# Four PSUM banks for scores and relu, three for maxima, with new orders; the last head projected with the last tile

## The chip, the cores and the metric

The kernel runs on one core of one Trainium2 chip. The metric is the device time of one execution in microseconds. PE stands for TensorE's matmuls and PEld for its weight loads, DVE for VectorE, ACT for ScalarE, POOL for GpSimd, and SP for the engine that issues most DMAs.

## The reference, cut to what matters

```python
def _A_ref(x, wqkv, wo):            # 32 heads, each with its own k and v, Dh = 18
    qkv = (x @ wqkv).reshape(B, S, 3, H, Dh)          # S = 2048, D = 576
    p = softmax(q k^T * Dh ** -0.5); o = p v
    return o.reshape(B, S, D) @ wo
def _B_ref(x, wq, wk, wv, wo):      # 32 heads of q, one k and one v for all
    ...
g = sigmoid((x * gate_w).sum(-1, keepdims=True))
return g * _A_ref(x, ...) + (1 - g) * _B_ref(x, ...)
```

Both parts see the same x. In the kernel they are 64 heads in a row: heads 0 to 31 are the B part, with k from ksb and v from vb, and heads 32 to 63 the A part, with k from ksa or ksb and v from vg.

## The kernel before, in words

The order of all instructions on each engine is the order in which the program is written out (a manual schedule). Tiles in PSUM come from pools that hand out banks in turn: ps_s with three banks (tiles ps), ps_m with four (tiles pm), and ps_o with the one bank acc. An instruction that writes a bank waits until the bank's last reader is done.

*First phase.* x and the weights are split into a high and a low part, and 56 projections (14 tiles of 128 weight columns by 4 stretches of 512 rows of x, `project`) of 14 matmuls each go to PSUM, three in ps and three in pm by turns, and are evicted to DRAM scaled by tv. `balance` works out tv from the sizes of the weights by a transpose (br to pm) and a small matmul (bd, two) on TensorE, once for the B part and once for the A part; `turn_mask` transposes a mask that it needs, and `shared_v` transposes v of the B part. `split_x` prepares further stretches of x. Then project_v makes v of the A part, beside the maxima of the first rows (the order LEADS).

*Second phase.* The loop runs over T in steps of two; T // 16 is the head, T % 16 the first of two tiles of 128 keys, A and B. A pass of the loop does for both tiles the scores of 4 stretches of 512 queries (sA0 to sB3, `step_scores`, 56 rows at partition 0, exponentials on ScalarE), the maxima of another head's rows 22 tiles ahead (mA0 to mB3, `step_max`, 54 rows at partition 64, reductions on VectorE), and the product of the exponentials of the pass before with v (`step_pv`, four matmuls of 19 columns side by side in acc): P or p and f for tile A, Q or h and H for tile B, whole (512 queries) or in halves of 256. Of the eight maxima of a pass one (mA1) is left out: x is a matmul with the difference of two stretches of k, ScalarE takes its relu, and VectorE adds it to mA0's scores and takes the maximum in one instruction (L519). x is made one pass ahead. So ScalarE reads nine tiles a pass, and VectorE seven. U is a unit of the output projection (`out_proj`): twelve matmuls of 288 columns into one bank, which ScalarE copies (first segment) or VectorE adds to oacc (later ones).

A pass takes one order string. Before a head's first pass, M and T stand at different heads: the row maxima of a head are put together by `max_rows` on VectorE ahead of the pass with T % 16 = 10. In the pass with T % 16 = 0 (END) the last product of a head is done and `head_out` copies acc on VectorE; the next pass is AFTER, and others are PLAIN. A pass with a unit due is UNIT, wherever it stands. ALONE is for the last passes (T from 1002), when no maxima are left.

Units come in segments: 32 units of the first four tiles of 128 rows of the heads' outputs (T 521 to 857, one or two a head), 32 of the next four (T 942 to 1008), and 32 short ones of three matmuls for the 110 rows of the ninth tile (T from 1021, the rest behind the loop). The last head's 18 rows are projected by `last_out`: acc is copied and split, stacked by DMAs into 54 rows, and multiplied in 32 matmuls, scaled by the reciprocal sums while VectorE adds to oacc. The rows of out leave by DMA, 16 in all.

## Time and profile before

| | |
|---|---|
| median of 3 runs | 2694.31 us (2694.18 to 2694.47) |
| the profiled execution's own time | 2694.18 us |
| its span in the profile | 2692.4 us |
| busy PE, DVE, ACT, POOL | 99%, 90%, 89%, 10% of the span |
| granted TensorE clock | 0.997, mean |
| stretch 300 to 1300 us: busy DVE, ACT | 98.1%, 98.8% |
| stretch 1432 to 2193 us: busy DVE, ACT | 93.5%, 95.7% |
| stretch 2449 to 2589 us: busy DVE, ACT | 83.7%, 80.3% |

The first two rows and the span are read together: the time of an execution lies 1.8 us over the span that its instructions fill. A busy share of PE of 99% says little, since matmuls are pipelined and their ends are modelled; start-to-start times say more. In rows of a timeline the columns are start, duration (us), engine, line, operation, output and inputs with shapes, count, and the idle time before with what ended it. In a chain of waits they are start, duration, and engine with what it did.

### The profile page before, as it was taken

How to read it: one execution, taken by the hardware profiler on the slowest of the kernel's cores; microseconds unless marked ns; L12 is line 12 of the kernel's file. 1: busy time of each engine (PE TensorE's matmuls, PEld its weight loads, DVE VectorE, ACT ScalarE, POOL GpSimd, SP SyncE). 2: the span in 40 equal slices, each digit the busy share in tenths (PEclk: the TensorE clock that was granted, in tenths of full speed). 3: DMA queues.
4: the chain of work that ended last, by engine and by line, in shares of the span. 5: the costliest groups of instructions: out<-in, count | busy, mean ns of one | idle time of the engine just before them, and what ended most of it. 6: DMA issues, size and time to landing. Idle time of an engine off the chain costs nothing.

```text
span 2692.4 us, 57950 instructions
## 1 busy us (share of the span) xinstructions
PE 2658.4 (99%) x22210; PEld 956.5 (36%) x22210; DVE 2428.6 (90%) x4616; ACT 2389.0 (89%) x4810; POOL 280.1 (10%) x520
## 2 busy tenths in 40 slices
PE   9999999999999999999999999999999999999999
PEld 6878322222222222222223333333333332223444
DVE  8347999999999999999999999999999999998865
ACT  4341899999999999999999999999999999998875
POOL 4740000002001100100110002000200011011000
PEclk9999999999999999999999999999999999999998
DMA  6332000011001100210132112112121212122312
GB/s 200 124 111 76 23 20 20 20 34 42 28 17 46 44 20 18 53 32 20 36 76 82 51 43 85 42 50 65 55 67 50 59 50 60 39 76 81 88 36 96
DMA packets 127089, 150.36 MB, mean 56 GB/s; under 512 B 55339, under 2 KB 94411, under 8 KB 125614
## 3 DMA queue, kind: packets, MB, share of 16 engines
q1 hardware_dynamic: 113628, 121.86, 16.0%
q0 software_dynamic: 7968, 19.23, 2.1%
q10 hardware_dynamic: 5216, 5.57, 0.6%
q8 instruction: 174, 2.85, 0.4%
q14 instruction: 103, 0.84, 0.1%
HBM read 90.89 MB, written 46.45 MB: 51 GB/s over the span
## 4 chain that ended last, share of the span: by engine, by line
ACT 53%; PE 35%; DVE 6%; DMA 2%; issue 2%; SPq 1%; POOL 0%; DVEq 0%; ACTq 0%; POOLq 0%
ACT pt L557 47%; PE acc L563 12%; PE ps L550 11%; ACT xb L516 6%; PE pm L679 4%; DVE mx L522 3%; PE pm L243 3%; PE ps L243 2%; PE ps L292 2%; PE pm L513 1%; SPq L56 1%; DVE oe L573 1%; DVE junk L519 1%; DMA oih<-onh 1%; DMA R<-r_d 1%
## 5 line engine op out<-in xcount | busy, mean ns | idle before, releaser
L557 ACT ACTIVATE pt<-ps 128x512 f32<-128x512 f32 x4052 | 2093.8, 639 | 64.6 <-PE pm L513 57.9
L522 DVE TENSOR_REDUCE mx<-pm 128x1 f32<-128x512 f32 x3094 | 1939.1, 682 | 86.9 <-PE pm L513 71.1
L550 PE MATMUL ps<-qs,ksb 56*128 56x512 f16 x2688 | 816.6, 379 | 12.0 <-ACT pt L557 0.6
L513 PE MATMUL pm<-ksb,qs 54*128 54x512 f16 x2363 | 737.2, 382 | 1.2 <-DVE mx L522 0.4
L563 PE MATMUL acc<-pt,vb 128*19 128x512 f32 (+1 forms) x6136 | 591.3, 457 | 1.9
L563 PE MATMUL acc<-pt,vg 128*19 128x256 f32 (+1 forms) x5664 | 579.5, 481 | 2.3 <-DVE oe L573 0.5
L513 PEld LDWEIGHTS <-qs 54*128 54x128 f16 x4096 | 330.5, 93 | 252.1 <-issue 195.3
L550 PE MATMUL ps<-qs,ksa 56*128 56x512 f16 x1364 | 404.4, 379 | 4.8 <-ACT pt L557 1.3
L550 PEld LDWEIGHTS <-ksb 56*128 56x128 f16 x2688 | 174.9, 94 | 616.2 <-issue 569.9
L513 PE MATMUL pm<-ksa,qs 54*128 54x512 f16 x1232 | 384.8, 382 | 0.6 <-ACT xb L516 0.4
L519 DVE CUSTOM_DVE_ANT_0 junk<-pm,xb 128x512 bf16<-128x512 f32 x501 | 340.5, 680 | 0.1
L516 ACT ACTIVATE xb<-pm 128x512 f32<-128x512 f32 x501 | 318.2, 635 | 0.4 <-PE pm L513 0.4
L550 PEld LDWEIGHTS <-ksa 56*128 56x128 f16 x1408 | 89.3, 94 | 328.8 <-issue 297.7
L532 POOL TENSOR_SCALAR mt<-mt 128x32 f32<-128x32 f32 x64 | 18.5, 288 | 1606.2 <-DVE mt L530 1606.2
L563 PEld LDWEIGHTS acc<-pt,vb 128*19 128x19 f32 x6136 | 103.9, 96 | 221.7 <-issue 204.6
L563 PEld LDWEIGHTS acc<-pt,vg 128*19 128x19 f32 x5664 | 96.0, 97 | 222.9 <-issue 205.0
L513 PE MATMUL pm<-kdb,qs 54*128 54x512 f16 x373 | 141.7, 380 | 0.0
L573 DVE COPY oe<-acc 128x512 f32<-128x512 f32 x63 | 43.6, 692 | 30.0 <-PE acc L563 26.9
L295 ACT ACTIVATE vst<-ps 128x288 f32<-128x288 f32 x32 | 13.1, 411 | 62.9 <-PE ps L292 62.9
L251 ACT ACTIVATE ph<-ps,tv 128x512 f16<-128x512 f32 x29 | 19.8, 686 | 50.4 <-PE ps L243 34.3
L251 ACT ACTIVATE ph<-pm,tv 128x512 f16<-128x512 f32 x27 | 18.4, 686 | 48.4 <-PE pm L243 35.7
L257 DVE SCALAR_TENSOR_TENSOR pl<-pm,tv,ph 128x512 f16<-128x512 f32 x27 | 20.1, 749 | 37.9 <-ACT ph L251 24.9
(150 smaller groups left out, 1505.5 us busy)
## 6 DMA issues: line engine op xcount, KB each, us to landing
qs<-qkh SPq DMA_DIRECT2D x244, 72.0 KB
qs<-qkl SPq DMA_DIRECT2D x122, 72.0 KB
onh<-oh SPq DMA_DIRECT2D x32, 256.0 KB
onl<-ol SPq DMA_DIRECT2D x32, 256.0 KB
oih<-onh SPq DMA_DIRECT2D x16, 512.0 KB
oil<-onl SPq DMA_DIRECT2D x16, 512.0 KB
ot<-oe SPq DMA_DIRECT2D x220, 36.0 KB
R<-r_d SPq DMA_DIRECT2D x55, 144.0 KB
```

The lines of the kernel that those rows point to most:

```text
L243: nc.tensor.matmul(fp[:, a0:b0], w[a][:kr, k, :], X[b][:kr, k, s0 + a0:s0 + b0], start=(n == 0), stop=(n == len(PROJ) - 1), skip_group_che ...
L251: nc.scalar.activation(h, fp, AF.Copy, scale=t)
L292: nc.tensor.matmul(fp[:, 0:288], X[b][:kr, k, st_ * P:(st_ + 1) * P], w[a][:kr, k, :], start=(n == 0), stop=(n == len(PROJ) - 1))
L513: nc.tensor.matmul(pm, qs[u % 3][b:b + 54, i * P:(i + 1) * P], k, start=True, stop=True)
L516: nc.scalar.activation(MX["x", u, i], pm, AF.Relu)
L519: nc.vector.tensor_tensor_reduce(junk, pm, MX.pop(("x", u, i)), 1.0, -3e38, op0=OP.add, op1=OP.max, accum_out=MX[u][:, i, c:c + 1])
L522: nc.vector.tensor_reduce(MX[u][:, i, c:c + 1], pm, axis=AX.X, op=OP.max)
L550: nc.tensor.matmul(ps, kst(u)[b:b + 56, i * P:(i + 1) * P], qs[u % 3][b:b + 56, c * 512:(c + 1) * 512], start=True, stop=True)
L557: nc.scalar.activation(pt, ps, AF.Exp, scale=SCALE / LIFT ** 2)
L563: nc.tensor.matmul(acc[32 * j:32 * j + 19, a:b], v_of(u, i), PT[u, i, j][:, a:b], start=(i == 0 and a == 0), stop=(i == 15), skip_group_ch ...
L573: nc.vector.tensor_copy(oe, acc)
L679: nc.tensor.matmul(fp[:, 0:288], o[b][:r, t, s2 * P:(s2 + 1) * P], w[a][:r, t, 288 * hf:288 * hf + 288], start=(n == 0), stop=(n == 3 * nt ...
```

## The change

ps_s has four banks and ps_m three. x and its relu take a bank of ps_s (`other`), and so do the mask, the v transposes and, in the lead, the maxima of stretch 3; in ALONE only stretch 0 of the scores uses ps_m. All orders but FIRST, ALONE and LEADS are new, two are added (UNIT_END for a unit at a head's end, UNIT2 for the second segment), and AFTER follows every head's end. The second segment's units are spread to T = 1016. The third segment is gone: the last head's outputs are divided, gated and split on the chip like the others, put by eight DMAs into the free rows of the ninth tile, and that tile is projected at the end by 96 matmuls of 128 rows, through seven banks in turn. Matmuls that nothing reads (`idle`) run on TensorE in the meantime. `normalise` of the ninth tile is spread over passes. In the first phase `balance` uses acc and stands in the middle of a projection's matmuls, `turn_mask` stands with the second of its steps, and `split_x` of the last stretches goes ahead by one projection.

```diff
-    ps_s = ctx.enter_context(tc.tile_pool(name="ps_s", bufs=3, space=PSUM))
-    ps_m = ctx.enter_context(tc.tile_pool(name="ps_m", bufs=4, space=PSUM))
+    ps_s = ctx.enter_context(tc.tile_pool(name="ps_s", bufs=4, space=PSUM))
+    ps_m = ctx.enter_context(tc.tile_pool(name="ps_m", bufs=3, space=PSUM))
...
+    def other():
+        return ps_s.tile([P, 512], F32, name="ps")
...
-        project(3, hold=True, gen=bal, at=(7,))
-        project(4, hold=True, gen=bal, at=(3,))
+        project(3, hold=True, gen=bal, at=(12,))
+        project(4, hold=True, gen=bal, at=(9,))
...
-            if n == 8:
+            if n == 7:
                 for c in (6, 7):
                     split_x(c)
...
-            project(n)
+            project(n, gen=bal, at={15: (7,), 16: (4,)}.get(n, ()))
...
-        pm = ps_m.tile([P, 512], F32, name="pm")
+        pm = other() if c == "x" or spare else ps_m.tile([P, 512], F32, name="pm")
...
-        ps = (ps_m if alone and c < 2 else ps_s).tile([P, 512], F32, name="pm" if alone and c < 2 else "ps")
+        ps = (ps_m if alone and c == 0 else ps_s).tile([P, 512], F32, name="pm" if alone and c == 0 else "ps")
...
+    def end_bank(n=[0]):
+        n[0] += 1
+        return ps_s.tile([P, 512], F32, name="ps") if n[0] % 7 < 4 else ps_m.tile([P, 512], F32, name="pm")
...
+        nc.scalar.activation(oe[:, 0:256], acc[:, 0:256], AF.Copy)
+        nc.vector.tensor_copy(oe[:, 256:512], acc[:, 256:512])
+        pt, pb = end_bank(), end_bank()
+        for c in range(4):
+            nc.tensor.transpose(pt[:, P * c:P * c + P], oe[:, P * c:P * c + P], ident)
+        idle(5)
...
+        nc.vector.tensor_tensor(o4, p4, r.rearrange("p (j c) -> p c j", c=4).unsqueeze(3).to_broadcast([P, 4, 4, 32]),
+                                op=OP.mult)
+        for c in range(4):
+            nc.tensor.transpose(pb[:, P * c:P * c + P], ot[:, P * c:P * c + P], ident)
+        idle(14)
+        nc.scalar.activation(oh, pb, AF.Copy)
+        nc.vector.tensor_tensor(ol, pb, oh.bitcast(F32), op=OP.subtract)
+        r0 = DH * (NU - 1) - 8 * P
+        for j in range(4):
+            dma(end["h"][r0:P, 512 * j:512 * j + 512], oh[32 * j:32 * j + DH, :])
+            dma(end["l"][r0:P, 512 * j:512 * j + 512], ol[32 * j:32 * j + DH, :], nc.scalar)
+        w = WO[8]
         for st_ in range(16):
             for hf in range(2):
...
+                fp = end_bank()
+                for n, (a, b) in enumerate(PRODS):
+                    nc.tensor.matmul(fp[:, 0:288], end[b][:, st_ * P:(st_ + 1) * P],
+                                     w[a][:, 0, 288 * hf:288 * hf + 288], start=(n == 0), stop=(n == 2))
+                dst = L["oacc"][:, st_, 288 * hf:288 * hf + 288]
+                nc.vector.tensor_tensor(dst, fp[:, 0:288], dst, op=OP.add)
+            dma(out[st_ * P:(st_ + 1) * P, :], L["oacc"][:, st_, :], nc.scalar if st_ % 2 else None)
...
-    SEG = ((0, [P] * 4, 450, 521, 857), (4, [P] * 4, 862, 942, 1008), (8, [DH * (NU - 1) - 8 * P], 950, 1021, 1034))
+    SEG = ((0, [P] * 4, 450, 521, 857), (4, [P] * 4, 862, 942, 1016))
...
-    PLAIN = "sA0 mA2 sA1 mA0 sA2 mA3 P sA3 mB0 sB0 mB1 sB1 mB2 h sB2 mB3 sB3 x H"
+    PLAIN = "mB1 mB3 sA0 sA1 mA3 sA2 P mB2 sA3 x sB0 mA2 sB1 mB0 h sB2 mA0 H sB3"
...
+    UNIT_END = "mB3 sA0 mA2 sA1 mA3 sA2 P sA3 mB1 sB0 mB2 Q x sB1 mA0 sB2 mB0 sB3 U"
...
-        order = LEADS if T < 0 else FIRST if T == 0 else ALONE if alone else UNIT if units else \
-            END if T % 16 == 0 else AFTER if order is END else PLAIN
+        order = LEADS if T < 0 else FIRST if T == 0 else ALONE if alone else (UNIT2 if T >= SEG[1][3] else UNIT_END if T % 16 == 0 else UNIT) if units else \
+            END if T % 16 == 0 else AFTER if T % 16 == 2 and T > 2 else PLAIN
```

Three places show how the rows move. First TensorE in a plain pass, before the change, from the second tile's first score (L550 writes a score, L513 a maximum, L563 is the product with v): sB0, mB1, sB1, mB2 and h.

```order
L550 LDWEIGHTS ksb_95
L550 MATMUL ps_8934<-qs1_93,ksb_95 128x512
L513 LDWEIGHTS qs2_94
L513 MATMUL pm_8938<-ksb_95,qs2_94 128x512
L550 LDWEIGHTS ksb_95
L550 MATMUL ps_8941<-qs1_93,ksb_95 128x512
L513 LDWEIGHTS qs2_94
L513 MATMUL pm_8945<-ksb_95,qs2_94 128x512
L563 MATMUL acc_100<-pt_8864,vb_97 19x256
```

The same place after it, TensorE, with lines five or fewer further down (L551 a score, L514 a maximum, or x where kdb is read, L564 the product): x, sB0, mA2, sB1, mB0 and h.

```order
L514 LDWEIGHTS qs0_92
L514 MATMUL ps_8969<-kdb_96,qs0_92 128x512
L551 LDWEIGHTS ksb_95
L551 MATMUL ps_8973<-qs1_93,ksb_95 128x512
L514 LDWEIGHTS qs2_94
L514 MATMUL pm_8977<-ksb_95,qs2_94 128x512
L551 LDWEIGHTS ksb_95
L551 MATMUL ps_8980<-qs1_93,ksb_95 128x512
L514 LDWEIGHTS qs2_94
L514 MATMUL pm_8984<-ksb_95,qs2_94 128x512
L564 MATMUL acc_100<-pt_8903,vb_97 19x256
```

x stood at the pass's end in a bank of pm and now stands ahead of the second tile in a bank of ps, and the last maximum ahead of h has no score beside it.

Second, TensorE behind the last scores, before the change: the halves and the whole of the last products with v (L563), with short units (L679) between them.

```order
L550 MATMUL ps<-qs_92,ksa_2753 128x512
L563 MATMUL acc<-pt,vg 19x256 x4
L679 MATMUL pm<-woh,endh 128x288
L679 MATMUL pm<-woh,endl 128x288
L679 MATMUL pm<-wol,endh 128x288
```

The same place after it, TensorE, up to the first idle matmul (L713 are the transposes in `last_out`, L707 is `idle`).

```order
L551 MATMUL ps<-qs_92,ksa_2749 128x512
L564 MATMUL acc<-pt,vg 19x256 x4
L564 MATMUL acc<-pt,vg 19x512 x4
L564 MATMUL acc<-pt,vg 19x256 x8
L713 MATMUL ps<-ident,oe 128x128 x4
L707 LDWEIGHTS qs_92
L707 MATMUL acc<-qs_92 128x512
```

The short units are gone from between the products; all projection of the ninth tile comes behind the second idle stretch.

Third, TensorE in the first phase before the change, in the fourth and fifth projections (L243): the mask (L164) ahead of them, the transpose of br (L206) behind seven matmuls, the small matmul (L214) behind three of the next projection.

```order
L164 MATMUL pm<-ident,mask_r 128x14 x4
L243 MATMUL pm<-xh,wh 128x512 x4
L243 MATMUL pm<-xh,wl 128x512 x3
L206 MATMUL pm<-ident,br 2x128
L243 MATMUL pm<-xh,wl 128x512
L243 MATMUL pm<-xl,wh 128x512 x4
L243 MATMUL pm<-xh,wh 128x512
L243 MATMUL pm<-xh,wl 128x512
L243 MATMUL pm<-xh,wh 128x512 x3
L214 MATMUL pm<-bd,two 128x2
```

And after it, TensorE (L248 the projections, L209 the transpose, L167 the mask, L219 the small matmul).

```order
L248 MATMUL pm<-xh,wh 128x512 x4
L248 MATMUL pm<-xh,wl 128x512 x4
L248 MATMUL pm<-xl,wh 128x512 x4
L209 MATMUL acc<-ident,br 2x128
L248 MATMUL pm<-xh,wh 128x512
L248 MATMUL pm<-xh,wl 128x512
L248 MATMUL pm<-xh,wh 128x512 x4
L248 MATMUL pm<-xh,wl 128x512 x4
L248 MATMUL pm<-xl,wh 128x512
L167 MATMUL ps<-ident,mask_r 128x14 x4
L219 MATMUL acc<-bd,two 128x2
```

The transpose stands five matmuls later, the small matmul six, and the mask is now turned directly ahead of it, in a bank of ps.

More of the change, by code (lines that the diff above doesn't have):

```diff
@@ L161, in turn_mask @@
     def turn_mask():
-        pt = ps_m.tile([P, 512], F32, name="pm")
+        pt = other()
         for g in range(4):
@@ L204, in balance @@
         yield
-        pt = ps_m.tile([P, 512], F32, name="pm")
+        pt = acc[:, 0:P]
         nc.tensor.transpose(pt[0:2, 0:P], r, ident)
@@ L212, in balance @@
         yield
-        pb = ps_m.tile([P, 512], F32, name="pm")
+        if g == 0:
+            turn_mask()
+        pb = acc[:, P:P + 2]
         nc.tensor.matmul(pb[:, 0:2], two, dg, start=True, stop=True)
@@ L276, in shared_v @@
         st = ST.pop(c)
-        pv = ps_m.tile([P, 512], F32, name="pm")
+        pv = other()
         for j in range(4):
@@ L791, in gated_mix_kernel @@
     FIRST = "sA0 mA2 sA1 mA0 sA2 mA3 sA3 mB0 sB0 mB1 sB1 mB2 sB2 mB3 sB3 x"
-    PLAIN = "sA0 mA2 sA1 mA0 sA2 mA3 P sA3 mB0 sB0 mB1 sB1 mB2 h sB2 mB3 sB3 x H"
-    UNIT = "sA0 mA2 sA1 mA0 sA2 mA3 P sA3 mB0 sB0 mB1 sB1 mB2 U sB2 mB3 sB3 x Q"
-    END = "sA0 mA2 sA1 mA3 sA2 mB0 P sA3 mB1 sB0 mA0 sB1 x Q sB2 mB2 sB3 mB3"
-    AFTER = "sA0 mA2 p sA1 mA0 sA2 mA3 sA3 x f sB0 mB0 sB1 mB1 h sB2 mB2 sB3 mB3 H"
+    PLAIN = "mB1 mB3 sA0 sA1 mA3 sA2 P mB2 sA3 x sB0 mA2 sB1 mB0 h sB2 mA0 H sB3"
+    UNIT = "mB2 sA0 mB0 sA1 mA0 P mB3 sA2 mA2 sA3 Q mA3 sB0 x sB1 mB1 sB2 U sB3"
+    END = "mA0 sA0 mB0 p mA2 sA1 x mB2 sA2 sA3 mA3 f sB0 mB1 mB3 sB1 sB2 Q sB3"
+    AFTER = "mB3 sA0 mB1 mB2 sA1 p sA2 x sA3 mB0 f mA0 sB0 mA3 sB1 h mA2 sB2 H sB3"
+    UNIT_END = "mB3 sA0 mA2 sA1 mA3 sA2 P sA3 mB1 sB0 mB2 Q x sB1 mA0 sB2 mB0 sB3 U"
+    UNIT2 = "sA0 mA3 sA1 mB0 sA2 P sA3 mB1 sB0 mB2 sB1 x U mA2 sB2 mA0 sB3 Q mB3"
     ALONE = "sA0 sA1 P U sA2 sA3 U sB0 sB1 h U sB2 sB3 H U"
@@ L843, in gated_mix_kernel @@
         run(slow.pop(0))
[L844 to L845 removed]
     pull(10 ** 9)
[L847 removed]
+    last_out()
 def kernel(A_x, A_wqkv, A_wo, B_x, B_wq, B_wk, B_wv, B_wo, gate_w):
```

61 lines of the change are left out of this document (14 added, 47 removed).

## The prediction

> **What bounds the kernel now.** I read the chain of waits first, in order of time, because it names what ended last. Most of its pieces from 280 us on are ScalarE's: the exponentials of L557 and the relu of L516.
>
> ```profile
> 332.72 0.49 ACT xb L516
> 333.21 3.92 ACT pt L557 x8
> ...
> 369.07 3.92 ACT pt L557 x8
> ```
>
> Eight exponentials and a relu are one pass of the loop, 3.92 + 0.49 = 4.41 us, 0.49 us a tile. A head is eight passes, 8 x 4.41 = 35.28 us, but from 333.21 to 369.07 are 35.86 us: 0.58 us of each head is not ScalarE's work. That is all that a plain head can give. Next I measured other heads, by stretches from one copy of acc (L573) to the next, with the share of that line alone.
>
> ```profile
> 1471.78:1508.97 37.19, 0.69 (x1) 1.00 0.11 31
> 1508.97:1547.56 38.59, 0.69 (x1) 1.00 0.23 59
> 2495.52:2542.12 46.60, 0.69 (x2) 1.00 0.29 87
> ```
>
> A head with one unit of the output projection takes 37.19 us, one with two 38.59, one with a unit in nearly every pass 46.60. So there are three kinds of head, and the first phase and the tail besides. TensorE issues all their work in order, so I costed the new orders by walking TensorE's queue by hand, with these durations from the timeline of one pass.
>
> ```profile
> 1020.15 1.05 PE L563 MATMUL acc<-pt,vb 128*19 128x512 f32 x8
> 1021.14 0.39 PE L550 MATMUL ps<-qs,ksb 56*128 56x512 f16 x1
> 1021.14 0.39 PE L513 MATMUL pm<-ksb,qs 54*128 54x512 f16 x1
> 1021.37 0.38 PE L550 MATMUL ps<-qs,ksb 56*128 56x512 f16 x1
> 1021.37 0.38 PE L513 MATMUL pm<-ksb,qs 54*128 54x512 f16 x1
> 1021.79 0.37 PE L550 MATMUL ps<-qs,ksb 56*128 56x512 f16 x1
> 1021.79 0.39 PE L513 MATMUL pm<-ksb,qs 54*128 54x512 f16 x1
> 1022.11 0.63 PE L563 MATMUL acc<-pt,vb 128*19 128x256 f32 x8
> 1022.67 0.39 PE L550 MATMUL ps<-qs,ksb 56*128 56x512 f16 x1
> ```
>
> Start to start: a whole P step takes 0.99 us (1020.15 to 1021.14), a half one (p, f, h, H) 0.56 (1022.11 to 1022.67). A score and a maximum start together, since they use different halves of the rows, and the next pair 0.23 later, or the P step 0.31 (0.32 at 1021.79). The pair at 1021.79 waited for a bank. How long a bank is held is in the timeline of a head's second plain pass, and of VectorE where the row maxima stand.
>
> ```profile
> 1007.98 0.39 PE L550 MATMUL ps<-qs,ksb 56*128 56x512 f16 x1
> ...
> 1008.40 2.56 ACT L557 ACTIVATE pt<-ps 128x512 f32<-128x512 f32 x5 [0.32 <-PE pm L513]
> ...
> 1019.02 0.68 DVE L522 TENSOR_REDUCE mx<-pm 128x1 f32<-128x512 f32 x1
> ...
> 1020.19 0.65 DVE L522 TENSOR_REDUCE mx<-pm 128x1 f32<-128x512 f32 x1
> ...
> 1021.37 3.08 DVE L522 TENSOR_REDUCE mx<-pm 128x1 f32<-128x512 f32 x5
> ```
>
> A waiting ScalarE starts 0.42 us after the matmul's start and 0.03 after its end, and a first exponential takes 2.56 - 4 x 0.49 = 0.60, so a tile is done 1.02 us after its matmul began; for the bank's way back I take 0.05. A maximum takes VectorE (3.08 - 0.68) / 4 = 0.60 us, a pass has seven, 4.2 of 4.41 us; once a head the row maxima put in (1020.19 - 1019.02) - 0.60 = 0.57. The row at 1008.40 is where a plain head loses most: with B banks, TensorE may turn away from the scores for 0.49 x (B + 1) - 1.02 - 0.05 from one score to the next before ScalarE runs dry. For B = 3 that is 0.89, and across a whole P step it is 0.31 + 0.99 = 1.30. Within plain passes the relu of x, in a bank of the other pool, fills that gap; behind a head's first pass it doesn't.
>
> **The change part by part.** *Plain passes.* Four banks carry nine tiles: B = 4 allows 1.38. The new PLAIN on TensorE: sB3 with mB1 at 0, mB3 with sA0 0.23, sA1 with mA3 0.44, sA2 0.66, P 0.97, sA3 with mB2 1.96, x with sB0 2.19, sB1 with mA2 2.40, mB0 alone 2.62, h 2.93, sB2 with mA0 3.49, H 3.80, next sB3 4.36. That is 4.36 against ScalarE's 4.41, where the old order adds up to 4.15 (0.75 + 0.99 + 0.75 + 0.56 + 0.54 + 0.56): one matmul more stands without a partner, paid from slack. Banks: sB1 needs the bank of sA2, free at 1.02 + 3 x 0.49 + 0.05 = 2.54, so it waits 0.14, but mB0 behind it may start only at 2.62 anyhow, in mA2's rows, so the wait is covered. If it weren't, sB1 at 2.54, then 0.22 + 0.31 + 0.56 + 0.31 + 0.56 = 1.96 make 4.50. For the maxima, three banks: mA3 needs the bank of mA0, free 0.1 us late, which sA2 beside it covers. I take 4.41, no change, with ends 4.41 and 4.50. Nothing can be gained, since ScalarE is full.
>
> *Heads' ends, plain heads.* END puts the P of the head's end last but one, so the copy of acc (0.69) starts about 1.1 us after it (0.99 and 0.1 of wait) and AFTER's p, which waits for it, is 0.13 late; the walk gives 4.48 for END and 4.48 for AFTER. The row maxima's 0.57 us reaches mB0 through three banks: 0.27 late, some 0.22 on ScalarE. So 6 x 4.41 + 2 x 4.48 + 0.22 = 35.64 against 35.86: -0.22 a head, bounds -0.58 (all hidden) and +0.3 (nothing hidden that was walked). There are 36 such heads (31 ahead of the first unit, 5 after the first 32 units): **-8 us**.
>
> *Heads with one or two units.*
>
> ```profile
> 2509.68 0.80 PE L679 MATMUL pm<-woh,oih 128*128 128x288 f32 x4
> ...
> 2511.47 0.39 PE L550 MATMUL ps<-qs,ksa 56*128 56x512 f16 x1
> ```
>
> A unit holds TensorE 1.79 us, more than four banks carry: UNIT_END and AFTER are TensorE's own sum, 6.02 + 4.38, and 0.2 because AFTER's mB2 gets the unit's bank, which ScalarE empties late: 10.6, with the 0.22 at the row maxima 10.8. Before it was 37.19 - 6 x 4.41 = 10.7. A second unit cost 38.59 - 37.19 = 1.40; UNIT stands in the pass of the row maxima and takes 5.8, or 6.1 where they delay mA2, so 1.2 to 1.5 over 4.41 + 0.22. I take +0.1 a head, bounds -1 and +0.5, 21 heads: **+2 us**.
>
> *Heads with a unit in each pass.* UNIT2 has the pairs and P steps of UNIT, so TensorE alone fills 46.60 / 8 = 5.83 us a pass in both, 1.42 more than a plain one. Spread to step 1016, four of the 32 units move behind step 1002, where the maxima are over: four pairs with switches 1.1, P steps 2.1 and the unit 1.79 make 5.0 against ScalarE's 3.92, 1.1 a unit. 4 x -0.3: **-1 us**.
>
> *Tail.*
>
> ```profile
> 2662.63 0.40 PE L679 MATMUL pm<-woh,endh 110*128 110x288 f32 x1
> ...
> 2663.62 0.63 PE L563 MATMUL acc<-pt,vg 128*19 128x256 f32 x8
> ...
> 2664.77 0.63 PE L563 MATMUL acc<-pt,vg 128*19 128x256 f32 x8
> ```
>
> ```profile
> L733 DVE SCALAR_TENSOR_TENSOR oacc<-pm,rl,oacc 128x288 f32<-128x288 f32 x32 | 13.7, 509 | 0.0
> L730 PE MATMUL pm<-wl,stk 54*128 54x288 f32 x32 | 13.0, 553 | 0.1
> L687 DVE TENSOR_TENSOR oacc<-pm,oacc 128x288 f32<-128x288 f32 x30 | 12.0, 452 | 4.7 <-PE pm L679 4.6
> ```
>
> ```profile
> L730 PE MATMUL pm<-wl,stk x32: 293/604/607, 2674.8 to 2687.4; 54*128 54x288 f32 x32
> qs<-qkh POOLq DMA_DIRECT2D x12, 72.0 KB, 2.7
> ```
>
> Before, short units (three matmuls; two of them 2663.62 - 2662.63 = 0.99, so 0.5 us each) stand between the last P steps. Ten fewer end the last P step, 2664.77 + 0.56 = 2665.3, some 3.5 us earlier, the rest of their 5 us lying beside ScalarE's work. Behind it 27.1 us are left of the span of 2692.4: mostly 20 additions of 12.0 / 30 = 0.40 us and 32 of 13.7 / 32 = 0.43 on VectorE, and the last transfer. The last addition follows the matmul at 2687.4 by 1.6, so the transfer out takes 3.4. After: copy 0.5, transposes 0.7, reciprocal and gate 0.5, product 0.7, transposes 0.7, oh and ol 1.4, transfer 2.7, some 7.3 us (estimates from the copy of 512 columns at 0.69, the exponential's 0.60, a start 0.42 behind a matmul, and the landing of small loads in the last row), in which TensorE does idle matmuls that nothing waits for. Then 32 additions at 0.40, 12.8, or 96 matmuls at (0.80 - 0.40) / 3 = 0.13 (the four of the row at 2509.68), 12.5, side by side; 0.5 for the last, 3.4 out: 24.0 against 27.1. So -3.5 - 3.1: **-6.6 us**, bounds -9 and 0.
>
> *First phase.*
>
> ```profile
> 65.98 0.27 PE L206 MATMUL pm<-ident,br 128*2 128x128 f32 x1 [0.70 <-DVE br L203]
> ```
>
> Here TensorE stands at a bank's start until br is there; with the transpose in mid bank that 0.70 goes. At the first balance five more matmuls stand ahead of the transpose, but the banks of the first projections come free only with tv, as late as before, and the v transposes and the mask now sit in the scores' pool too, so the seventh projection gets its bank one eviction later; splitting x earlier pays for that. **-1 us**, bounds -3 and +2.
>
> Sum, on the profiled execution of 2694.18 us (span 2692.4), which lies 0.13 under the runs' median: -8 + 2 - 1 - 6.6 - 1 = -14.6, **2680 us**.
>
> **A rule that speaks against it.**
>
> ```profile
> 1021.15 0.10 PEld L550 LDWEIGHTS <-ksb 56*128 56x128 f16 x1
> ```
>
> This load for the next score began 0.01 us after the score of 1021.14 on the same rows, and the next score followed 0.23 later: loading hides behind a matmul in the same rows. The Trainium skill (TensorE: Matmul & The Clock Gate, What overlaps and what doesn't) says that weights load during a running matmul only where the row group differs; this trace disagrees, for pairs at least. If the rule held for mB1 mB3 and sA0 sA1, where two of one kind stand in a row, the time would be the last rival's.
>
> **The rivals.** *The bank of sB1 holds up the pass* (slower): if mB0 starts only a slot after sB1, a plain pass is 4.50, as worked out. It decides from 0.05 us on, the slack between 4.36 and 4.41. Some 340 plain passes (six in each of 58 heads, less 11 with UNIT) x 0.09 = +31: 2711 us. For it: five switches of that loop are known to 0.02 each. Against: s and m matmuls start together in every pair. Chance 0.18.
>
> *Nothing in the heads moves*: ScalarE is full, and each 0.1 us won at an end is lost at the row maxima. Then tail and first phase alone: 2694 - 8.5 = 2686 us. Chance 0.17.
>
> *All bubbles hidden*: 36 x -0.58 and 21 x -0.6, with the rest -8.5: 2652 us. For it: B = 4 covers every gap that I walked. Against: the copy's wait and 0.57 us on VectorE stay. Chance 0.12.
>
> *The clock falls in the tail*: the matmuls of L730 took 604 ns in the middle against 293 at best, while TensorE mostly waited. With 96 matmuls at twice 0.13 the last part takes 25 us, not 12.7: 2692 us, no change. The idle matmuls speak against it. Chance 0.05. The Trainium skill (same page, Part 1) puts the fall after an idle window of about 3.4 us, which the new wait of some 3 us would barely miss.
>
> *Weights in a row aren't hidden*: two loads of 0.10 (row 1021.15) a pass, less 0.05 of slack, 0.15 x 340 = +51: 2731 us. Chance 0.04.
>
> **How the numbers follow.** The forecast keeps 0.44. Range 2655 to 2712: down to short of all bubbles hidden, up to the bank's case; outside lie the last rival, some 0.08 of all bubbles hidden and some 0.06 of the bank's case, whose loop may be longer than worked out. Faster by over 0.2% (5.4 us, about what a measurement of this kernel can tell from no change) means under 2688.9: 0.42 of 0.44, 0.13 of 0.17, and 0.12, in all 0.67; within 0.2%: the clock's 0.05 and 0.05 from the edges of the first two; slower, the bank's 0.18, the last 0.04 and 0.01 of an edge: 0.23.
>
> **What would show it.** Right: plain heads of 35.5 to 35.7 us by the copies of acc, plain passes at 4.41 of exponentials without gaps; heads with units within 0.3 us of before; the last P step's end 3 to 4 us nearer and 24 us ahead of the end. Wrong: ScalarE waiting in each plain pass for sB3, sA0 or sA1 (bank case), heads of 35.3 or less (all hidden), L735's matmuls over 0.2 us apart (clock).

## The result, and the profile after

The changed kernel takes 2686.11 us (median of 8 runs, 2684.89 to 2688.33), the kernel before 2694.5 us beside it (8 runs, 2694.18 to 2696.34): a ratio of 0.9969, 95% interval 0.996 to 0.9978. The forecast was 2680 with a range of 2655 to 2712. So the sign and the range held, and of the 14.6 us that were forecast 8.4 came.

The profiled execution of the changed kernel took 2688.33 us, with a span of 2686.0. A second profile of the same kernel, taken with the experiments as *changed_again*, has a span of 2684.5. Both stand below, since they differ in the tail.

The chain of waits of the changed kernel, by engine and by line:

```profile
PE 84%; DVE 12%; issue 2%; DMA 1%; ACT 1%; SPq 0%; DVEq 0%; POOL 0%; ACTq 0%; POOLq 0%
PE acc L564 35%; PE ps L551 20%; PE pm L514 14%; DVE mx L523 7%; PE pm L678 4%; PE ps L514 3%; PE pm L248 3%; PE ps L248 2%; PE ps L297 2%; DVE junk L520 2%; DVE oe L574 1%; ACT pt L558 0%; SPq L56 0%; DVE oacc L738 0%; DVE norm_a L190 0%
```

The exponentials have left the chain: L558 holds 0% of it, and TensorE 84%, with VectorE's maxima next to it. The sum of the prediction rested on ScalarE as the bound, so this is the first thing that it had wrong.

Where the 8 us came from is read from copy to copy of acc, as in the prediction. Before the change, the stretches with the copy's line alone (start and end, length, the copies' busy time and count, clock, DMA share, GB/s) are these: the heads before the first unit, the heads with one and two units, and the last five copies.

```profile
318.11:1432.21 1114.10, 21.44 (x31) 1.00 0.12 33
1432.21:2266.47 834.26, 15.22 (x23) 1.00 0.20 58
2410.77:2631.31 220.54, 3.45 (x5) 1.00 0.24 72
```

The same after the change, with one plain head besides (the second row):

```profile
317.94:1429.57 1111.63, 21.44 (x32) 1.00 0.12 33
1034.92:1070.68 35.76, 0.69 (x1) 1.00 0.07 19
1429.57:2262.48 832.91, 15.07 (x22) 1.00 0.20 58
2406.15:2626.16 220.01, 3.42 (x5) 1.00 0.24 71
```

And in the second profile, *changed_again*, where the heads repeat to within 0.04 us a stretch:

```profile
317.64:1429.24 1111.60, 21.45 (x31) 1.00 0.12 33
1429.24:2262.19 832.95, 15.08 (x23) 1.00 0.20 58
2405.85:2625.86 220.01, 3.44 (x6) 1.00 0.24 72
```

The rest is the tail. The chain behind the last scores of *changed_again*, in order of time:

```profile
2656.64 3.13 PE acc L564 x32
...
2664.52 2.51 DMA endl<-ol
...
2667.08 0.54 PE ps L735 x2
...
2667.65 12.76 DVE oacc L738 x32
```

The last P step ends at 2656.64 + 3.13 = 2659.77, 24.7 us ahead of the span's end. In the first profile it is this:

```profile
2656.95 3.13 PE acc L564 x32
...
2664.83 2.52 DMA endl<-ol
...
2667.39 0.71 PE ps L735 x2
2668.10 2.16 PE pm L735 x9
2670.26 0.73 PE ps L735 x3
...
2671.02 11.23 DVE oacc L738 x28
```

There it ends at 2660.08, 25.9 us ahead of the end, and between the transfer and the additions stand 3.6 us of L735's matmuls on the chain, not 0.5. Put together, against the span before (2692.4, the last P step's end at 2665.3):

| part of the span | forecast | first profile | second profile |
|---|---|---|---|
| up to the first copy | -1 | -0.2 | -0.5 |
| 31 plain heads, and four more to the copy at 2406 | -8 | -2.5 - 0.6 | -2.5 - 0.6 |
| heads with one or two units | +2 | -1.3 | -1.3 |
| heads with a unit in each pass, to the last copy | | -0.5 | -0.5 |
| last copy to last P step's end (34.0 before, 33.9 after) | -1 - 3.5, with the row above | -0.1 | -0.1 |
| behind the last P step (27.1 before) | -3.1 | -1.2 | -2.4 |
| sum | -14.6 | -6.4 | -7.9 |

Three terms are off by more than 3 us. For the plain heads 5 us too much gain was forecast, for the last passes 3.9 too much, and for the heads with one or two units 3.3 too little. These misses partly cancel, so that the sum came nearer than its terms. The experiments ask why.

### The profile page after: what moved, and what is told of

Same layout as the page of the kernel before. It is cut to its first block, busy times and chain, and to the rows that moved or that the text cites. A ratio compares the mean times of both kernels' runs of the same rounds, so it can differ in the third digit from the quotient of the medians.

```text
span 2686.0 us, 59393 instructions
## 1 busy us (share of the span) xinstructions
PE 2665.6 (99%) x22697; PEld 905.2 (34%) x22697; DVE 2428.2 (90%) x4586; ACT 2402.0 (89%) x4810; POOL 278.8 (10%) x518
## 4 chain that ended last, share of the span: by engine, by line
PE 84%; DVE 12%; issue 2%; DMA 1%; ACT 1%; SPq 0%; DVEq 0%; POOL 0%; ACTq 0%; POOLq 0%
PE acc L564 35%; PE ps L551 20%; PE pm L514 14%; DVE mx L523 7%; PE pm L678 4%; PE ps L514 3%; PE pm L248 3%; PE ps L248 2%; PE ps L297 2%; DVE junk L520 2%; DVE oe L574 1%; ACT pt L558 0%; SPq L56 0%; DVE oacc L738 0%; DVE norm_a L190 0%
## 5 line engine op out<-in xcount | busy, mean ns | idle before, releaser
L558 ACT ACTIVATE pt<-ps 128x512 f32<-128x512 f32 x4074 | 2109.1, 645 | 64.7 <-PE ps L551 47.0
L523 DVE TENSOR_REDUCE mx<-pm 128x1 f32<-128x512 f32 x3072 | 1918.4, 682 | 70.9 <-PE pm L514 34.5
L551 PE MATMUL ps<-qs,ksb 56*128 56x512 f16 x2688 | 810.5, 380 | 0.0
L514 PE MATMUL pm<-ksb,qs 54*128 54x512 f16 x2341 | 768.2, 381 | 1.9 <-DVE mx L523 0.6
L564 PE MATMUL acc<-pt,vb 128*19 128x512 f32 (+1 forms) x6392 | 598.5, 446 | 1.8
L564 PE MATMUL acc<-pt,vg 128*19 128x256 f32 (+1 forms) x5904 | 585.7, 468 | 1.2 <-DVE oe L574 0.5
L514 PEld LDWEIGHTS <-qs 54*128 54x128 f16 x4096 | 292.1, 94 | 598.0 <-issue 532.5
L551 PE MATMUL ps<-qs,ksa 56*128 56x512 f16 x1386 | 412.1, 380 | 0.7
L514 PE MATMUL pm<-ksa,qs 54*128 54x512 f16 x1232 | 401.4, 380 | 2.2 <-DVE mx L523 1.2
L551 PEld LDWEIGHTS <-ksb 56*128 56x128 f16 x2688 | 198.3, 93 | 402.5 <-issue 370.9
L517 ACT ACTIVATE xb<-ps 128x512 f32<-128x512 f32 x501 | 310.5, 620 | 7.7 <-PE ps L551 7.3
L564 PEld LDWEIGHTS acc<-pt,vb 128*19 128x19 f32 x6392 | 108.3, 96 | 248.1 <-issue 232.0
L564 PEld LDWEIGHTS acc<-pt,vg 128*19 128x19 f32 x5904 | 100.7, 97 | 231.4 <-issue 223.9
L551 PEld LDWEIGHTS <-ksa 56*128 56x128 f16 x1408 | 100.3, 94 | 203.9 <-issue 186.7
L514 PE MATMUL ps<-kdb,qs 54*128 54x512 f16 x373 | 141.0, 378 | 0.1
L686 DVE TENSOR_TENSOR oacc<-pm,oacc 128x288 f32<-128x288 f32 x32 | 14.6, 458 | 49.1 <-PE pm L678 49.1
```

What stands on the lines that cost most here:

```text
L514: nc.tensor.matmul(pm, qs[u % 3][b:b + 54, i * P:(i + 1) * P], k, start=True, stop=True)
L517: nc.scalar.activation(MX["x", u, i], pm, AF.Relu)
L523: nc.vector.tensor_reduce(MX[u][:, i, c:c + 1], pm, axis=AX.X, op=OP.max)
L551: nc.tensor.matmul(ps, kst(u)[b:b + 56, i * P:(i + 1) * P], qs[u % 3][b:b + 56, c * 512:(c + 1) * 512], start=True, stop=True)
L558: nc.scalar.activation(pt, ps, AF.Exp, scale=SCALE / LIFT ** 2)
L564: nc.tensor.matmul(acc[32 * j:32 * j + 19, a:b], v_of(u, i), PT[u, i, j][:, a:b], start=(i == 0 and a == 0), stop=(i == 15), skip_group_ch ...
```

## The experiments

Ratios are to the kernel before on the same chip, with 95% intervals. The pitch of a single pass, where it is given, is the time from the first exponential of a pass to that of the next, from the starts in the trace. For a plain head it reads, from END on:

| kernel | END | AFTER | the five other passes | pass of the row maxima | head |
|---|---|---|---|---|---|
| before | 4.36 | 4.48 | 4.77, 4.44, 4.41, 4.54, 4.44 | 4.41 | 35.86 |
| changed | 4.73 | 4.51 | 4.37, 4.36, 4.41, 4.38, 4.37 | 4.62 | 35.76 |

The forecast walked 4.48, 4.48, five of 4.41, and 4.63. So AFTER and the row maxima were right to 0.03, the plain passes are 0.03 shorter than ScalarE was thought to allow, and END is 0.25 longer.

**The head's end: another order (*end_order*).** On VectorE, END begins with a wait, and from then on there is none (the copy's line is L574):

```profile
1030.71 0.69 DVE L520 CUSTOM_DVE_ANT_0 junk<-pm,xb 128x512 bf16<-128x512 f32 x1 [0.17 <-PE pm L514]
...
1031.33 3.67 DVE L523 TENSOR_REDUCE mx<-pm 128x1 f32<-128x512 f32 x6
1034.92 0.69 DVE L574 COPY oe<-acc 128x512 f32<-128x512 f32 x1
```

On TensorE in the same place stand mB2, sA3, mA3 and f:

```profile
1031.59 0.38 PE L514 MATMUL pm<-ksb,qs 54*128 54x512 f16 x1
1031.72 0.37 PE L551 MATMUL ps<-qs,ksb 56*128 56x512 f16 x1
1032.07 0.37 PE L514 MATMUL pm<-ksb,qs 54*128 54x512 f16 x1
1032.37 0.63 PE L564 MATMUL acc<-pt,vb 128*19 128x256 f32 x8
```

mA3 starts 0.35 behind sA3. It takes the bank of mB0, whose maximum is the first of the six at 1031.33 and lasts 0.68, to 1032.01; mA3 starts 0.06 later, and all that follows in the queue, f and the second tile's scores, is late by a good 0.2. The edit puts f there:

```diff
-    END = "mA0 sA0 mB0 p mA2 sA1 x mB2 sA2 sA3 mA3 f sB0 mB1 mB3 sB1 sB2 Q sB3"
+    END = "mA0 sA0 mB0 p mA2 sA1 x mB2 sA2 sA3 f mA3 sB0 mB1 sB1 mB3 sB2 Q sB3"
```

> Only END is changed: f ahead of mA3, and mB1 and mB3 each beside a score. First theory: a head's end takes 4.73 us and not 4.48 because mA3 waits some 0.25 for one of three banks of maxima on TensorE. Then END falls to about 4.5, plain heads from 35.76 to 35.5, 36 of them, about 2678 us. Rival: VectorE is the bound at a head's end (14 maxima of 0.60 and the copy of 0.69 fill 9.1 of the 9.24 us of the two passes). Then heads keep 35.7 or more and the time lies within 3 us of the changed kernel's 2686.

Measured: 2687.85 us, ratio 0.9973 (0.9961 to 0.9984). END fell to 4.52, as the first theory said, but AFTER rose from 4.51 to 4.72, and the head stayed. Its row of a plain head, and TensorE's next wait for VectorE:

```profile
1034.54:1070.30 35.76, 0.68 (x1) 1.00 0.07 19
```

```profile
1035.28 0.63 PE L564 MATMUL acc<-pt,vb 128*19 128x256 f32 x8 [0.21 <-DVE oe L574]
```

p of AFTER now waits 0.21 for the copy, which stands on VectorE behind the maxima that came later. The wait was moved, not removed: the rival's outcome.

**The copy in halves, and the copy made short.** If VectorE sets the two passes, taking the copy from it must show. *copy_halves* gives ScalarE one half:

```diff
-        nc.vector.tensor_copy(oe, acc)
+        nc.scalar.activation(oe[:, 0:256], acc[:, 0:256], AF.Copy)
+        nc.vector.tensor_copy(oe[:, 256:512], acc[:, 256:512])
```

> ScalarE copies one half of acc at each head's end and VectorE the other. First theory: VectorE sets the time of END and AFTER (14 maxima of 0.60 and the copy of 0.61 start to start, 9.0 of 9.24 us); with 0.25 to 0.3 taken off it plain heads fall from 35.76 to 35.5, 8 to 12 us in all. Rival: p waits for the later half, and ScalarE's stands behind the exponentials of its queue, so the wait of TensorE for the copy grows from 0.13 and the head's end stays at 9.24 or more.

Measured: 2699.19 us, ratio 1.0012 (1.0003 to 1.0021), a plain head 36.04, AFTER 4.78. The copy of one bank by two engines went one behind the other:

```profile
1038.69 0.46 ACT L574 ACTIVATE oe<-acc 128x256 f32<-128x256 f32 x1
...
1039.18 0.42 DVE L575 COPY oe<-acc 128x256 f32<-128x256 f32 x1 [0.45 <-ACT oe L574]
...
1039.66 0.63 PE L564 MATMUL acc<-pt,vb 128*19 128x256 f32 x8 [0.32 <-DVE oe L575]
```

VectorE stood 0.45 us until ScalarE was done, and p waited longer than before. So this run answers the rival's way, but tells nothing of VectorE's load. *short_copy*, which leaves out 448 of the copy's 512 columns, does:

```diff
-        nc.vector.tensor_copy(oe, acc)
+        nc.gpsimd.memset(oe[:, 64:512], 1.0)
+        nc.vector.tensor_copy(oe[:, 0:64], acc[:, 0:64])
```

> Left out: of acc only 64 of 512 columns are copied at a head's end, the others are filled with ones by GpSimd, so VectorE's copy falls from 0.69 to under 0.2 us. First theory: VectorE sets the time of END and AFTER (9.0 of 9.24 us), and plain heads fall from 35.76 to 35.4 or less. Rival: the loss at a head's end is in TensorE's order and its waits for banks; only p's 0.13 us of wait for the copy goes, heads of 35.6 or more.

Measured: 2676.56 us, ratio 0.993 (0.9918 to 0.9943). The copy's row is 0.22 us, and a plain head is this:

```profile
1029.64:1065.23 35.59, 0.22 (x1) 1.00 0.07 19
```

0.47 us less on VectorE gave 0.17 a head: END stayed at 4.73, AFTER fell to 4.42 to 4.46, the pass of the row maxima to 4.55. The value is the rival's, 35.6. So VectorE's load isn't the whole bound at a head's end: END's wait for mA3's bank lies ahead of the copy and is untouched by it. Both runs together suggest that END's 0.25 needs two cures at once, an order in which no maximum stands where its bank isn't free, and a shorter copy behind it; one alone was given back (*end_order*) or left END as it was (*short_copy*). The two together weren't run, so this is not shown.

**Banks and orders apart.** Three kernels keep the new tail and the new order of the first phase, and put back the banks, the orders of the second phase, or both. The first edit puts back the banks (with x, the mask, the v transposes and the lead's maxima in ps_m again), the second the orders, of which PLAIN is shown:

```diff
-    ps_s = ctx.enter_context(tc.tile_pool(name="ps_s", bufs=4, space=PSUM))
-    ps_m = ctx.enter_context(tc.tile_pool(name="ps_m", bufs=3, space=PSUM))
+    ps_s = ctx.enter_context(tc.tile_pool(name="ps_s", bufs=3, space=PSUM))
+    ps_m = ctx.enter_context(tc.tile_pool(name="ps_m", bufs=4, space=PSUM))
...
-    PLAIN = "mB1 mB3 sA0 sA1 mA3 sA2 P mB2 sA3 x sB0 mA2 sB1 mB0 h sB2 mA0 H sB3"
+    PLAIN = "sA0 mA2 sA1 mA0 sA2 mA3 P sA3 mB0 sB0 mB1 sB1 mB2 h sB2 mB3 sB3 x H"
```

> The changed kernel with the orders of before: banks four and three, with x in a bank of scores at the pass's end. First theory: banks alone give no gain; with old orders the maxima come in bunches that three banks don't hold, so plain passes lose, plain heads are over 36 us. Rival: four banks for scores give the gain by themselves, ScalarE's 0.477 us a tile allows 4.30 a pass, and plain heads fall under 35.7.

Measured: 2724.42 us, ratio 1.0109 (1.0095 to 1.0123). A plain head and a head with a unit in nearly each pass:

```profile
1041.06:1077.22 36.16, 0.69 (x1) 1.00 0.07 18
2571.84:2620.76 48.92, 0.69 (x1) 1.00 0.18 48
```

> The new orders with three banks for scores and four for maxima, x in the latter. First theory: the orders need the fourth bank of scores; TensorE waits for a score's bank across P in each plain pass, 4.41 + 0.1 or more, heads over 36.3, while END falls below 4.73 and the heads with a unit in each pass keep the row maxima hidden (45.3). Rival: the orders alone make the gain and the banks nothing: plain heads 35.6 to 35.8.

Measured: 2842.8 us, ratio 1.0549 (1.0535 to 1.0563). The same two heads:

```profile
1090.95:1129.41 38.46, 0.69 (x2) 1.00 0.06 17
2692.64:2739.59 46.95, 0.68 (x2) 1.00 0.18 50
```

A plain pass is 4.84. END is 4.94 and the heads with a unit in each pass 46.9, where under 4.73 and 45.3 had been expected. Neither half of the change is a gain by itself: against the kernel before, the new orders with the old banks lose 2.6 us a plain head, and the new banks with the old orders 0.3 a plain head and 2.3 a head with a unit in each pass. The last of the three has the old banks and the old orders, with the new tail.

> The changed kernel with three banks for scores and four for maxima, x in the latter, and the orders of before: the new tail and first phase alone. First theory, from the copies of acc: heads gave about 5 us of the 8.4, so 2691. Rival, the forecast's terms: the tail and first phase alone gave 8, so 2686 to 2687.

Measured: 2688.96 us, ratio 0.9977 (0.9968 to 0.9986): between the two expectations. Its last five copies, and a plain head:

```profile
1036.57:1072.44 35.87, 0.69 (x2) 1.00 0.07 19
2410.80:2627.10 216.30, 3.46 (x6) 1.00 0.24 73
```

This is the surprise. Up to the copy at 2410.80 it loses 4.6 us to the changed kernel (2406.15), but in the next five heads it is 3.7 us shorter (216.30 against 220.01). With the old banks and orders, taking units out of these heads pays 220.54 - 216.30 = 4.2 us; with the new ones it paid 0.5. What banks and orders gain in the plain heads, they lose there almost whole.

**Units to step 1008 (*units_to_1008*).**

```diff
-    SEG = (..., (4, [P] * 4, 862, 942, 1016))
+    SEG = (..., (4, [P] * 4, 862, 942, 1008))
```

> Only the second segment's units end at T = 1008 again. First theory: a unit behind step 1002 costs 1.15 us there, and the passes freed of it in heads 59 to 62 give some 0.1 to 0.4 back only, since the row maxima show once the unit is gone: three to four units, about 2 us less, 2684. Rival, the forecast's step: a unit costs 1.42 in a pass with maxima and 1.1 behind, so 1 us more, 2687.

Measured: 2684.36 us, ratio 0.9959 (0.9947 to 0.9972). The last five copies, and the last P step:

```profile
2405.55:2626.92 221.37, 3.43 (x5) 1.00 0.24 71
```

```profile
2653.73 3.13 PE acc L564 x32
```

By the formula of `due`, four units fewer stand behind step 1002. From the last copy to the last P step's end are 29.9 us, not 33.9. That is three of the four units; the fourth stands in the pass of T = 1008 ahead of the last copy, and delays that copy by 1.2 us from the pass's first exponential (3.9 against 2.7). So the four cost 4.0 + 1.2 = 5.2 us there, 1.3 each (1.1 was forecast). In the heads ahead, they cost only 221.37 - 220.01 + 1.2 = 2.6, so 0.65 each, where 1.42 was forecast. Spreading them was a loss of 2.6 us from the copy at 2406 to the last P step's end; the ratios, 0.9959 against 0.9968 of *changed_again*, agree in size, but their intervals overlap.

**Why a unit is worth so little there.** A pass with a unit is 5.79 to 5.80 in both kernels, as walked. But the pass with the row maxima (T % 16 = 10) takes 6.2 in *units_to_1008* and 5.8 before. In the changed kernel a pass just ahead of one without a unit (T = 968, 984 and 998) takes 6.2 too, and where both meet, at T = 954, it is 6.65. One theory was that the unit borrows one of three banks of maxima. *unit_in_scores* gives it one of the scores':

```diff
-                    fp = ps_m.tile([P, 512], F32, name="pm")
+                    fp = ps_m.tile([P, 512], F32, name="pm") if first or L["alone"] else other()
```

> The second segment's units take a bank of the scores' pool and not of the maxima's (behind step 1002 as in the changed kernel). First theory: heads 59 to 62 keep 46.5 us although units were taken out of them, because with three banks, one of them lent to the unit, VectorE has no maxima queued when it puts the row maxima together, and the pass takes 6.2 to 6.7 and not 5.8. Then these heads fall to 45.3, as with four banks for maxima: 4 x 1.2, about 5 us less, a ratio of 0.995. Rival: the row maxima delay these passes whatever the unit's bank, since three is too few for the maxima alone: 46.4 and no change. A second rival: the unit in a bank of the scores holds ScalarE up, which has its own slack of 1.4 us a pass there: no change either, but with gaps of ScalarE in all passes.

Measured: 2693.49 us, ratio 0.9993 (0.9984 to 1.0002). The passes of 6.2 to 6.65 take 6.5 to 6.6 now, and the others with a unit rise to 6.1. TensorE waits for the unit's bank:

```profile
2501.06 0.80 PE L678 MATMUL ps<-woh,oih 128*128 128x288 f32 x4 [0.25 <-ACT pt L558]
```

The theory fell. In *all_units_in_scores* the first segment's units do the same.

> Units of both segments take a bank of the scores' pool. First theory: as with the second segment alone, and AFTER behind a unit falls from 4.98 to about 4.5, since mB2 no longer gets the bank that ScalarE empties late: 21 x 0.4, 8 us less, so some 13 us with the second segment. Rival: the unit's copy then keeps a score's bank, and the score behind it waits as long: AFTER stays near 5.0 and nothing is won in heads 32 to 52.

Measured: 2700.36 us, ratio 1.0019 (1.001 to 1.0028). Behind a unit AFTER fell only to 4.84, and UNIT_END rose from 5.58 to 5.90: heads with one unit lost 0.2, with two 0.55.

The two kernels above that have one half of the change each say more. T = 970 is a pass without a unit in them, in *old_banks_orders* and in the changed kernel. With the passes before and behind it, it takes:

| banks for scores and maxima | orders | T = 968, 970, 972 | three passes with a unit |
|---|---|---|---|
| 3 and 4 | old | 5.80 + 4.62 + 5.74 = 16.2 | 17.4 |
| 4 and 3 | old | 6.33 + 4.72 + 5.96 = 17.0 | 19.0 |
| 4 and 3 | new (changed) | 6.23 + 5.28 + 5.69 = 17.2 | 17.8, with the row maxima (*units_to_1008*) |
| 3 and 4 | new | 6.51 + 5.22 + 6.01 = 17.7 | 17.4, without row maxima |

With the old orders a pass without its unit gives back 1.2 and 1.9 us, whichever pool has four banks; with the new ones 0.6, and next to nothing with four banks for the maxima. So it is the new orders, a PLAIN pass between two UNIT2 passes, that keep the unit's time, and not the count of banks for the maxima. Which of their rows does it wasn't tried.

**Row maxima at the unit (*rows_at_unit*).** In a pass with a unit VectorE waits 0.9 us for the unit's last matmul:

```profile
2500.51 0.46 DVE L686 TENSOR_TENSOR oacc<-pm,oacc 128x288 f32<-128x288 f32 x1 [0.89 <-PE pm L678]
```

This kernel puts the row maxima into that gap, ends the segment at 1008, and makes 18 idle matmuls.

```diff
-        if M >= 16 and M % 16 == 0 and M // 16 - 1 < NU:
-            max_rows(M // 16 - 1)
...
+        rows = [M // 16 - 1] if M >= 16 and M % 16 == 0 and M // 16 - 1 < NU else []
+        if rows and not units:
+            max_rows(rows.pop())
...
             elif k == "U":
+                if rows:
+                    max_rows(rows.pop())
```

> The changed kernel with 18 idle matmuls, the second segment to T = 1008, and the row maxima moved, in passes with a unit, from the pass's start to just ahead of the unit's addition, where VectorE waits 0.9 us for TensorE. First theory: 1.2 less from the clock, 3 from the segment, 0.44 in each of heads 59 to 62, and 0.3 in 11 heads with two units: 9 us less than the changed kernel, about 2677. Rival: behind the unit the row maxima only stand in the way of other maxima that TensorE waits for, and these passes stay at 6.2: 4 us less, 2682.

Measured: 2680.18 us (5 runs), ratio 0.9946 (0.9934 to 0.9959), the fastest here of those that leave nothing out, and 6 us below *changed_again* on the same chip. A head with two units, and one with a unit in each pass:

```profile
1500.63:1538.97 38.34, 0.69 (x2) 1.00 0.19 48
2532.49:2579.11 46.62, 0.68 (x1) 1.00 0.23 64
```

With all units in their heads, the pass of the row maxima is 5.80: the 0.44 is gone, so 46.62 stands here against 47.04 of *units_to_1008*. Heads with two units gain 0.23. So with three banks the row maxima can be hidden, here where VectorE waits anyway. The 9 us that were expected were not reached; the gain from the idle matmuls, counted as 1.2, is in doubt, as the next run shows.

**The clock in the tail (*idle_18*).** In the first profile the clock fell behind the transfer (stretch, length, PE, PEld, DVE, ACT, POOL busy, granted clock):

```profile
2667.40:2671.00 3.60, 3.60 (x15) 3.60 (x16) 1.83 (x4) 0.00 (x0) 0.00 (x0) 0.53 0.38 122
```

Fourteen matmuls of L735 lie 0.24 us apart there. Ahead of them TensorE had stood for 0.96 us, from L735's first matmul to the transfer's landing:

```profile
2666.43 0.40 PE L735 MATMUL ps<-woh,endh 128*128 128x288 f32 x1
2667.39 0.47 PE L735 MATMUL ps<-woh,endl 128*128 128x288 f32 x1 [0.56 <-DMA endl<-ol]
```

```diff
-        idle(14)
+        idle(18)
```

> Only the second stretch of idle matmuls is longer, 18 and not 14, so that they end (0.22 us each) when the last transfer lands. First theory: the clock halved for 3.6 us because TensorE stood still for some 0.9 us. Then the first matmuls of L735 lie 0.13 us apart, the last addition comes 1.4 us sooner, 2684.7 us. Rival: the clock falls whatever TensorE did, because of the change to full matmuls or because idle matmuls of 54 rows don't count as work: 0.24 us apart for 3.6 us as before, 2686 us.

Measured: 2685.32 us (2685.18 to 2685.56), ratio 0.9963 (0.9949 to 0.9977). The clock stayed up, and the matmuls are 0.13 apart; the same stretch reads:

```profile
2667.40:2671.00 3.60, 3.60 (x29) 3.60 (x29) 3.60 (x10) 0.00 (x0) 0.00 (x0) 1.00 0.73 257
```

This alone would say that the first theory holds. But the changed kernel itself, run again, kept its clock too, with 14 idle matmuls and the same standstill of 0.95 us.

> The changed kernel itself, to compare with the other kernels on one chip: a ratio of 0.9969, within 0.001.

Measured: 2686.13 us (2685.35 to 2688.15), ratio 0.9968 (0.9957 to 0.9979). The stretch from L735's first matmul:

```profile
2666.00:2669.60 3.60, 3.04 (x21) 2.71 (x21) 1.95 (x5) 0.00 (x0) 0.00 (x0) 1.00 0.35 91
```

Of the eleven profiles with 14 idle matmuls, the clock fell in three (the first profile, *end_order* and *copy_halves*), of the two with 18 in none. Where it falls, the additions end 1.5 us later, measured from L735's first matmul (15.8 against 14.3). Two profiles without a fall can't settle that 18 prevent it. Nor does a fall need the whole standstill: in *end_order* it began at 2666.69, 0.70 after L735's first matmul.

The same fall stands at the start of the second phase, in six of the fourteen profiles, both of the changed kernel among them. There the matmuls of 54 and 56 rows ahead of it lie at most 0.54 us apart, start to start. In the first profile:

```profile
281.65:285.06 3.41, 3.41 (x16) 0.53 (x15) 2.01 (x4) 2.50 (x6) 0.00 (x0) 0.50 0.00 0
```

A fall there costs 1.1 to 1.5 us: from the first exponential to the first copy of acc are 40.3 to 40.7 us in the kernels with the new banks and orders where it fell, and 39.2 where it didn't. Of the eight runs of the changed kernel, the two with a mean clock of 0.998 took 2687.63 and 2688.33 us, the six with 0.999 or 1.0 at most 2686.32. So a difference of 1 us between two kernels here can be the clock's.

## Why the prediction was right, and where not

The time moved the way that was forecast and lies in the range, but few of the terms held, and that their misses partly cancel is luck. Of the prediction's own signs, the heads with one or two units mostly stayed within 0.3 us of before, as it said; plain heads of 35.76 lie outside its 35.5 to 35.7, and the last P step's end is no nearer to the last copy.

*The bound.* The step "3.92 + 0.49 = 4.41 us, 0.49 us a tile", with its conclusion "Nothing can be gained, since ScalarE is full", failed. ScalarE's next tile starts 0.48 behind the one before when it has one waiting:

```profile
1006.44 0.59 ACT L517 ACTIVATE xb<-ps 128x512 f32<-128x512 f32 x1
1006.92 4.04 ACT L558 ACTIVATE pt<-ps 128x512 f32<-128x512 f32 x8
```

The starts in the trace lie 0.477 apart, which makes 4.30 a pass; the 0.49 of the chain was an average that held short waits, hidden in the rows' durations of 0.6. Plain passes now take 4.37, and that is the walk of TensorE's queue: 4.36 had been added up. So the walk was right and the ceiling above it was not. It gave 0.15 a head more than the forecast.

*Plain heads, -0.22.* They gave -0.10. Row maxima were forecast at 4.63 and took 4.62, AFTER 4.48 and 4.51. END took 4.73, not 4.48: the walk let mA3 start at its turn, and VectorE hadn't freed the bank. The prediction had asked when the maxima's banks come free in a plain pass and at the row maxima, but not in END, where they wait.

*Heads with one or two units, +0.1.* Inside a head the walk was right: UNIT_END and AFTER 5.59 + 4.98 = 10.57 against 10.6, UNIT 6.12 against "5.8, or 6.1". They gained 0.06 a head all the same, since their other passes are 4.37 and not 4.41 or more: a head with one unit gains 0.11, one with two 0.01, for UNIT took about 5.7 before.

*Heads with a unit in each pass, -1.* A unit of 1.42 us was to be saved ahead of step 1002 and 1.1 paid behind. 1.3 was paid and 0.65 saved. The price behind was mis-sized because a pass without a unit takes 3.8 there and not 3.92, the 0.49 a tile again. The failed step ahead is that a pass without its unit goes back to a plain one: it does with the old orders (heads 59 to 62 are 5.4 us shorter for four units in *old_banks_orders*, 1.35 each), but with the new ones the passes beside it take longer. Besides, the row maxima came out of cover, 0.4 a head even with all units in place (*units_to_1008*). The prediction looked at TensorE alone there, since the row maxima cost nothing before.

*Tail, -6.6.* Without the short units the last passes are shorter, as said: 29.9 us from the last copy to the last P step's end in *units_to_1008*, against 34.0 before, which is 4.1 where 3.5 was forecast. But the units now behind step 1002 take them back, so the last P step's distance from the last copy stayed at 34. Behind it, 24.0 was forecast and 24.7 came where the clock stayed up: 7.3 to the first full matmul (7.3 forecast), the additions 12.76 (12.8 forecast), and the last transfer 4.1 rather than 3.4 and a start. Where it fell, 25.9.

*First phase, -1.* The first copy of acc comes 0.2 and 0.5 us earlier in the two profiles, but that hides two things. The first exponential starts 2.4 us earlier (277.22 and 277.31 against 279.68). Of this, 0.8 is lost up to the first copy, and a further 1.1 to 1.5 through the fall of the clock shown above; in *idle_18* and *rows_at_unit*, where it didn't fall there, the first copy comes at 316.55 and 316.21, 1.6 and 1.9 ahead of before. And the 2.4 are not the forecast's: TensorE's standstill for br, 0.70 before, grew.

```profile
67.47 0.27 PE L209 MATMUL acc<-ident,br 128*2 128x128 f32 x1 [1.34 <-DVE br L206]
```

The projections end only 0.1 to 0.2 earlier. The time came in project_v beside the first maxima, 77.2 us before and 74.9 after, a step that the sum didn't have. It needs the new banks: with the old ones and the same order of the first phase it stays at 77.2 (*old_banks_orders*).

*The rivals.* "The bank of sB1 holds up the pass" did not come: the plain pass is 4.37, not 4.50. "Nothing in the heads moves" named 2686, which is the time measured, but not its cause: the heads gave about 5 us of the 8, the tail 1 to 2.5. "All bubbles hidden" needed heads of 35.3. "The clock falls in the tail" came in part, for 3.4 us in some runs and not for 25. "Weights in a row aren't hidden" fell: behind mB1 comes mB3 on the same rows of TensorE, 0.22 later, which is what a pair takes.

```profile
1012.28 0.39 PE L514 MATMUL pm<-ksb,qs 54*128 54x512 f16 x1
...
1012.29 0.10 PEld L514 LDWEIGHTS <-qs 54*128 54x128 f16 x1
...
1012.50 0.38 PE L514 MATMUL pm<-ksb,qs 54*128 54x512 f16 x1
```

The Trainium skill (TensorE: Matmul & The Clock Gate, What overlaps and what doesn't) lets a weight load overlap only where the row group differs; the load for the second of these two maxima on one row group began 0.01 us behind the first's start and took 0.10, and the second maximum still followed 0.22 behind the first, so this trace disagrees.

## What to carry to other kernels

When several engines are nearly full, walk every queue against every pool, and ask for each tile of the pool that gets smaller when its bank comes free: the bank given to the scores was missing for the maxima, at heads' ends and at row maxima that had cost nothing. Test banks and orders crosswise, since what looked like a lack of banks in the heads with units was the orders' doing. A rate read from a chain of waits is an upper bound of an engine's time per tile; take it from back-to-back starts where the engine has work waiting. When work is moved out of a pass, look at what it had been covering, and put uncovered work where an engine waits anyway, as was done with the row maxima at the unit.

## What the runs showed of the hardware

The clock halved for 3.4 us at a time (0.50 in the row from 281.65) in two places. In the tail it did so in three profiles of eleven, within or behind a standstill of at most 0.96 us, with idle matmuls of 54 rows ahead of it; at the start of the second phase in six of fourteen, with matmuls of 54 and 56 rows at most 0.54 us apart. (One more fall, in *copy_halves*, came behind 2.28 us between two matmuls.) The Trainium skill (TensorE: Matmul & The Clock Gate, Part 1: The HAM clock gate) has the clock set by free-running windows of some 3.4 us, which would fit a fall that comes in some executions only and lasts as long as a window. It puts the fall after an idle window of that length, and the trace differs there: TensorE wasn't idle for so long ahead of any of these. Whether matmuls of few rows count for less wasn't tried.

Two copies of different halves of one bank, by ScalarE and by VectorE, ran one after the other in *copy_halves* (0.46, then 0.42 after a wait of 0.45). The changed kernel's tail copies acc by the same two instructions, and there too VectorE starts 0.04 us behind ScalarE's end. The profile names ScalarE's copy as what released VectorE's in both; whether the chip needs that order or only this program asks for it wasn't tried.

The span ends 3.7 to 5.0 us behind the last addition in the profiles with the new tail, with the same transfers in all of them: a spread of 1.3 us, as much as some of the edits here move.
